# A fused pooled-attention and two-MLP kernel: chunk order, softmax subtraction on VectorE, and 24 idle weight steps

## The chip, the cores and the metric

The kernel runs on one core of one Trainium2 chip. The metric is the device time of one execution in microseconds; the number compared is the median over runs. The engines are named as the profile names them: PE is TensorE, DVE is VectorE, ACT is ScalarE, POOL is GpSimd, and SP is the queue that issues the DMAs.

## The reference

All data are float32. Keys and values are averaged over groups of 8 positions, attention runs over the 72 pooled positions, and the result passes through a gated MLP and an ELU MLP.

```python
k_p = k.reshape(B, H, Sp, pool, D).mean(axis=3)          # B 8, H 8, S 576, pool 8, Sp 72, D 64
v_p = v.reshape(B, H, Sp, pool, D).mean(axis=3)
scores = scale * np.matmul(q, k_p.transpose(0, 1, 3, 2))
scores = scores - np.max(scores, axis=-1, keepdims=True)
attn = np.exp(scores)
attn = attn / (np.sum(attn, axis=-1, keepdims=True) + 1e-09)
x = np.matmul(attn, v_p)                                 # -> (4608, 512)
gate = 1.0 / (1.0 + np.exp(-(x @ w_gate)))               # w_gate, w_val (512, 1536)
x = (gate * (x @ w_val)) @ w_out                         # w_out (1536, 512)
h = x @ w_in                                             # w_in (512, 2048)
g = np.where(h > 0.0, h, np.exp(np.minimum(h, 0.0)) - 1.0)
out = g @ w_out2                                         # w_out2 (2048, 512)
```

## The kernel before, in words

The MLP weights arrive as 64-bit words and are rebuilt on the chip as float32. Every float32 operand of a large product is then split into a rounded high half (an ACT copy) and a low half (a POOL or DVE subtraction), and a product is three matmul passes of those halves. The 4608 tokens are worked on in nine blocks of 512 (four tiles of 128). Each engine executes its instructions in the order in which the code emits them, so an instruction that waits holds up everything behind it on its engine.

**Block 0** does its attention first. Then comes the **chunk stage**: a loop over `c` from 0 to 5, each round handling one chunk of 128 columns of the first MLP for block 0, and beside it the attention of block 1, tile by tile. In a round PE does the scores of tile t (`emit_s`, name `ats`), the gate product (`gv`), the transposes of the softmax of the tile before (`emit_t`, name `att`), the value product (`gv`), the transposes of the next queries (`emit_q`, name `atq`) and the output products of the chunk before (`acc`). The names `ats`, `att` and `atq` share one PSUM place (tag `two`, one buffer of two banks): each must be read out before the next may be written. `convert(n)` takes n steps in the rebuilding of the first MLP's weights, each made of four DVE instructions (lines 116, 126, 130 and 120), an ACT copy and magnitude, and a POOL subtraction; there are three in a round.

The softmax of these tiles before the change: DVE finds the maximum of each head (line 612), ACT turns it into a bias (618) and then takes eight exponentials, one per head, straight from the PSUM bank (620). `emit_norm` then sums (DVE 628), adds a constant (ACT 636), inverts (DVE 637), scales the leftover window `pl` (DVE 640) and scales the whole tile (POOL 643).

After a stretch of gates for blocks 0 and 1 together comes the **bank stage**: the output products of block 1, with the attention of block 2 woven in by a hand-written table of half steps (`TURNS`, `put2`), through the same single `two` place.

The **middle stage** (blocks 2 to 8) runs seven products per half chunk: `u` counts half chunks from 0 to 11 and `k` the seven products. The product k=1 (`s2`) and the product k=3 (`s1`) write the same bank, and between them DVE must add the former into `u2` (line 1419). At even `u` the key sums of a later block (`pool_k`, line 490) are emitted at k=0. `WORK_AT` lists the places (u, k) where one step of the generator `prepared` is taken; it rebuilds the second MLP's weights (DVE lines 116 to 130 and 351 to 356, ACT copies and the magnitude at line 308, POOL subtractions, stores to DRAM from tiles named `nt`). Blocks 3 to 8 take the softmax in another form: DVE subtracts the maximum from the bank into SBUF (lines 598 and 599) and ACT takes one exponential in place (1206).

After block 8 the second MLP runs to the end.

Of the kernel before, what the change touches and what calls it, by code (L numbers as in the profile page):

```python
# [12 lines left out]
AF = mybir.ActivationFunctionType  # L13
# [11 lines left out]
def fused_kernel(  # L25
# [267 lines left out]
    def prepared():  # L293
# [44 lines left out]
        for q in range(C2 // 2):  # L338
# [31 lines left out]
            yield  # L370
            yield
            magnitude(i + 2)
# [7 lines left out]
        for i in range(C2, len(loads)):  # L380
            steps = narrowing(i)
            next(steps)
            if last is not None:
                keep(i - 1, *last)
            yield
            yield from steps
            fetch(i + 2)
            last = plain_t().bitcast(F32), tiles[i].bitcast(F32)
            apart(*last)
            yield  # L390
            magnitude(i + 1)
            yield
# [210 lines left out]

    peaks = {}

    def emit_s(t, p=None):
        a = two_banks("ats")
        scores(a, t, range(HP), q_t.pop(t))
        p = wts.tile([P, HK], F32, name="p0", tag="tt", bufs=2) if p is None else p
        sc = a[:, :, 0:4 * SP].rearrange("p a (h k) -> p a h k", k=SP)  # L610
        mx = at_p.tile([P, H], F32, name="mx", tag="mx", bufs=2)
        nc.vector.tensor_reduce(out=mx.rearrange("p (a h) -> p a h", a=2), in_=sc, op=ALU.max, axis=AX.X)
        peaks[t] = sc, mx
        return p

    def emit_exp(t, p):
        sc, mx = peaks.pop(t)
        nc.scalar.activation(out=mx, in_=mx, func=AF.Copy, scale=-SCALE)
        for h in range(H):
            nc.scalar.activation(  # L620
                out=p[:, h * SP:(h + 1) * SP], in_=sc[:, h // 4, h % 4], func=AF.Exp, scale=SCALE, bias=mx[:, h:h + 1]
            )
# [177 lines left out]
    with tc.manual_schedule():  # L800
# [43 lines left out]

        def scored(t):
            emit_s(t, ph[t])
            emit_exp(t, ph[t])

        for c in range(3):
# [5 lines left out]
        emit_k(0)  # L855
        scored(0)
        emit_q(3, qt[:, 3])
        scored(1)
        for t in range(2, TPW):
            scored(t)  # L860
            emit_norm(t - 2, ph[t - 2])
# [46 lines left out]
        for c in range(LAG_FROM):  # L908
            t = TPW + c - 1
            p = emit_s(t) if 0 < c <= TPW else None  # L910
            if c == 0:
                convert(1)
            gps = emit_gate(x0, c, 0)
            if c == 0:
                emit_k(1)
            if p is not None:
                emit_exp(t, p)
            sg = emit_sig(gps)
            if c:
                convert(1)  # L920
            if p is not None:
                emit_norm(t, p)
            if 1 < c <= TPW + 1:
                emit_t(t - 1)
            vps = emit_gate(x0, c, 1)
            if c < TPW:
# [3 lines left out]
            convert(1)  # L930
            g = emit_g(sg, vps)
            for op in post[c]:
                op()
# [91 lines left out]
        for i, (hq, hs, ht) in enumerate(TURNS):  # L1025
# [3 lines left out]
            put2(hs, s2, t)  # L1029
            put2(hs + 1, lambda t=t: emit_exp(t, p2[t]))  # L1030
            put2(hs + 2, lambda t=t: emit_norm(t, p2[t]))
# [172 lines left out]

        def exp_thin(p):
            nc.scalar.activation(out=p, in_=p, func=AF.Exp, scale=SCALE)

        halves_of = {}
# [15 lines left out]
        def thin_plan(m):  # L1224
# [9 lines left out]
            for i in range(TPW):  # L1234
# [4 lines left out]
                put(u + 1, 1, ready, AF.Exp)  # L1239
                put(u + 1, 2, lambda t=t: exp_thin(p_new[t]))  # L1240
                put(u + 1, 3, ready, AF.Sigmoid)
# [32 lines left out]
        SHAPE_AT = (0, 3)  # L1274
        WORK_AT = {(u, k) for u in range(2, C1, 2) for k in (0, 2, 3, 4, 5, 6)}
        WORK_AT |= {(u, k) for u in range(3, C1, 2) for k in (2, 4)}
# [422 lines left out]
```

## Time and profile before

| What | Value |
|---|---|
| median of three runs | 1864.53 us (1863.04 to 1865.72) |
| the profiled execution, its own time | 1861.72 us |
| its span, first to last instruction | 1859.9 us |
| PE busy in the span | 1783.1 us, 96% |
| DVE, ACT, POOL busy | 1082.1, 870.7 and 638.9 us |
| mean granted TensorE clock | 0.992 of full speed |

The profiled execution lies 1.8 us above its span and 2.8 us under the median. PE is busy for nearly the whole span, so the shares of busy time tell little; the stretches in which PE is not busy are what a reader looks for, and they lie in the first 330 us and in blocks 2 to 5.

### The profile page before, as it was taken

How to read it: one execution, taken by the hardware profiler on the slowest of the kernel's cores; microseconds unless marked ns; L12 is line 12 of the kernel's file. 1: busy time of each engine (PE TensorE's matmuls, PEld its weight loads, DVE VectorE, ACT ScalarE, POOL GpSimd, SP SyncE). 2: the span in 40 equal slices, each digit the busy share in tenths (PEclk: the TensorE clock that was granted, in tenths of full speed). 3: DMA queues.
4: the chain of work that ended last, by engine and by line, in shares of the span. 5: the costliest groups of instructions: out<-in, count | busy, mean ns of one | idle time of the engine just before them, and what ended most of it. 6: DMA issues, size and time to landing. Idle time of an engine off the chain costs nothing. (4 is left out here: it accounts for less than half of the span.)

```text
span 1859.9 us, 28508 instructions
## 1 busy us (share of the span) xinstructions
PE 1783.1 (96%) x10308; PEld 1581.6 (85%) x10308; DVE 1082.1 (58%) x2041; ACT 870.7 (47%) x1871; POOL 638.9 (34%) x626
## 2 busy tenths in 40 slices
PE   6679997999999999999999999999999999999999
PEld 5568776898988888899898989999999899999997
DVE  5687975776876767777664454345344444443432
ACT  4553444554544545455453244454444544544443
POOL 2354555443443434344332222222222222222222
PEclk9889999999999999999999999999999999999999
DMA  7345556876858677687666765353343343433431
GB/s 211 122 136 173 190 171 231 279 264 223 270 196 270 232 241 257 199 285 259 218 209 226 265 224 189 119 187 119 119 183 106 131 166 112 182 117 138 153 119 54
DMA packets 160013, 351.05 MB, mean 189 GB/s; under 512 B 48512, under 2 KB 86400, under 8 KB 159872
## 3 DMA queue, kind: packets, MB, share of 16 engines
q1 hardware_dynamic: 159872, 349.22, 55.1%
q8 instruction: 82, 1.34, 0.3%
q14 instruction: 59, 0.48, 0.1%
HBM read 288.88 MB, written 60.29 MB: 188 GB/s over the span
## 5 line engine op out<-in xcount | busy, mean ns | idle before, releaser
L1530 PE MATMUL bank<-form,wr 128*128 128x384 f32 x2016 | 411.0, 338 | 1.0 <-DVE u L1563 0.7
L1530 PEld LDWEIGHTS bank<-form,wr 128*128 128x128 f32 x2016 | 366.5, 188 | 29.1 <-DVE u L1563 1.1
L738 PE MATMUL acc<-g,wos 128*128 128x512 f32 x1128 | 354.3, 398 | 1.0 <-ACT g L96 0.2
L1576 PE MATMUL oacc<-w2o,gc 128*128 128x512 f32 x1080 | 288.9, 393 | 0.4 <-POOL gc L97 0.4
L1576 PEld LDWEIGHTS oacc<-w2o,gc 128*128 128x128 f32 x1080 | 199.6, 187 | 30.4 <-POOL gc L97 0.8
L97 POOL TENSOR_TENSOR gc<-ea,gc 128x384 fp32r<-128x384 f32 x96 | 98.0, 1021 | 298.7 <-ACT gc L96 295.6
L738 PEld LDWEIGHTS acc<-g,wos 128*128 128x128 f32 x1128 | 184.4, 189 | 11.4 <-ACT g L96 2.8
L97 POOL TENSOR_TENSOR gc<-pair,gc 128x384 fp32r<-128x384 f32 x96 | 97.8, 1018 | 260.6 <-ACT gc L96 240.1
L97 POOL TENSOR_TENSOR g<-sg,g 128x512 fp32r<-128x512 f32 x98 | 135.3, 1398 | 102.4 <-ACT g L96 102.2
L1404 PEld LDWEIGHTS pl<-s,wg 128*128 128x128 f32 x1008 | 139.9, 189 | 26.9 <-DVE u L1419 13.0
L1404 PE MATMUL pl<-s,wg 128*128 128x256 f32 x1008 | 153.6, 287 | 8.9 <-DVE u L1419 7.5
L1404 PE MATMUL pl<-s,tt 128*128 128x256 f32 x1008 | 152.1, 287 | 3.7 <-DMA tt<-td 2.9
L1404 PE MATMUL pl<-a,wg 128*128 128x256 f32 x1008 | 152.6, 287 | 3.0 <-DVE xe L1098 2.9
L1404 PEld LDWEIGHTS pl<-a,wg 128*128 128x128 f32 x1008 | 137.7, 189 | 16.4 <-ACT r L1104 5.8
L1404 PEld LDWEIGHTS pl<-s,tt 128*128 128x128 f32 x1008 | 139.2, 190 | 14.6 <-DVE rt L1344 2.0
L96 ACT ACTIVATE g<-sg 128x512 fp32r<-128x512 f32 x98 | 61.7, 630 | 180.2 <-DVE sg L1444 144.1
L1576 PE MATMUL oacc<-w2p,gc 128*128 128x512 f32 x540 | 143.1, 393 | 0.0
L1576 PEld LDWEIGHTS oacc<-w2p,gc 128*128 128x128 f32 x540 | 99.8, 187 | 14.8
L1539 ACT ACTIVATE ea<-bank 128x384 f32<-128x384 f32 x48 | 23.6, 492 | 157.7 <-PE bank L1530 157.7
L1543 DVE SCALAR_TENSOR_TENSOR ea<-ea,bank 128x384 f32<-128x384 f32 x48 | 26.6, 554 | 117.2 <-ACT ea L1540 117.2
L709 PE MATMUL gv<-x,wg 128*128 128x512 f32 x288 | 77.4, 420 | 10.0 <-POOL wg L97 6.0
L1539 ACT ACTIVATE pair<-pair 128x384 f32<-128x384 f32 x48 | 25.2, 525 | 129.6 <-DVE pair L1560 129.6
(223 smaller groups left out, 3059.5 us busy)
## 6 DMA issues: line engine op xcount, KB each, us to landing
wr<-wd SPq DMA_DIRECT2D x96, 896.0 KB, 5.2
tt<-td SPq DMA_DIRECT2D x84, 768.0 KB, 4.8
wos<-wd SPq DMA_DIRECT2D x94, 512.0 KB, 5.4
rw<-in_moe_w_out_dram SPq DMA_DIRECT2D x22, 512.0 KB, 3.7
td<-tw SPq DMA_DIRECT2D x36, 256.0 KB, 3.3
r<-yd SPq DMA_DIRECT2D x24, 384.0 KB, 8.2
out_dram<-po SPq DMA_DIRECT2D x36, 256.0 KB, 2.0
rw<-in_moe_w_in_dram SPq DMA_DIRECT2D x16, 512.0 KB, 7.1
```

The costliest lines, as they stand in the source:

```text
L96: nc.scalar.activation(out=dst_hi, in_=src, func=AF.Copy)
L97: eng.tensor_tensor(out=dst_lo, in0=src, in1=f32(dst_hi), op=ALU.subtract)
L709: nc.tensor.matmul(d, lhsT=w[:, i, a_w, j], rhs=x[j][:, a_x], start=(j == 0 and a_w == 0 and a_x == 0), stop=(j == KD - 1 and a_w == 1),)
L738: return lambda: nc.tensor.matmul(acc[m], lhsT=w[:, a_w, m * P:(m + 1) * P], rhs=g[:, a_g], start=(first and a_w == 0 and a_g == 0), stop= ...
L1404: nc.tensor.matmul(src, lhsT=w(a_w, j), rhs=f_t[nm][:, j, a_x], start=opens and m == 0, stop=m == 5, skip_group_check=True,)
L1530: nc.tensor.matmul(bank[b ^ flip], lhsT=wp[q][a_w][:, w, j * P:(j + 1) * P], rhs=form_tile(s, a)[j][:, a_x], start=opens and n == 0, stop= ...
L1539: nc.scalar.activation(out=e, in_=src, func=AF.Relu, scale=-1.0)
L1543: nc.vector.scalar_tensor_tensor(out=e, in0=e, scalar=-1.0, in1=src, op0=ALU.add, op1=ALU.max)
L1576: return lambda: nc.tensor.matmul(acc[t + i], lhsT=g[c][:, a_g, i * P:(i + 1) * P], rhs=wo2[2 * q + e][a_w], start=opens and p == 0, stop= ...
```

## The change

It has four parts.

1. In the chunk stage the order of a round is new. From c=2 on, the transposes of the former tile's softmax come first, then the gate product, a `convert`, the scores, the sigmoid, the value product, the exponential and the next queries; `emit_norm` now stands behind `emit_g`.
2. `emit_s` (block 1 and block 2) subtracts the maximum on DVE from the bank into SBUF, in one instruction of 128x576 elements, and `emit_exp` is one ACT instruction in place. The eight exponentials from the bank stay for block 0 only, under the name `straight`.
3. `prepared` loses 24 steps in which it did nothing: one in each of the 8 column pairs and one in each of the 16 row chunks.
4. `WORK_AT` loses the place k=0 at the five even `u`: 38 places in a block instead of 43.

```diff
@@ prepared()
             fetch(i + 3)
             yield
             yield
-            yield
             magnitude(i + 2)
             yield
...
             apart(*last)
-            yield
             magnitude(i + 1)
             yield
@@ emit_s, emit_exp
     def emit_s(t, p=None):
         a = two_banks("ats")
         scores(a, t, range(HP), q_t.pop(t))
         p = wts.tile([P, HK], F32, name="p0", tag="tt", bufs=2) if p is None else p
+        off_peak(p, a, 2)
+        return p
+
+    def emit_exp(p):
+        nc.scalar.activation(out=p, in_=p, func=AF.Exp, scale=SCALE)
@@ for c in range(LAG_FROM):
             t = TPW + c - 1
-            p = emit_s(t) if 0 < c <= TPW else None
-            if c == 0:
+            if c > 1:
+                emit_t(t - 1)
+            if c < 2:
                 convert(1)
             gps = emit_gate(x0, c, 0)
             if c == 0:
                 emit_k(1)
+            if c > 1:
+                convert(1)
+            p = emit_s(t) if 0 < c <= TPW else None
+            sg = emit_sig(gps)
+            vps = emit_gate(x0, c, 1)
             if p is not None:
-                emit_exp(t, p)
-            sg = emit_sig(gps)
-            if c:
-                convert(1)
-            if p is not None:
-                emit_norm(t, p)
-            if 1 < c <= TPW + 1:
-                emit_t(t - 1)
-            vps = emit_gate(x0, c, 1)
+                emit_exp(p)
             if c < TPW:
                 emit_q(t + 1)
             if c == 0:
                 sums_of("v", 1)
             convert(1)
             g = emit_g(sg, vps)
+            if p is not None:
+                emit_norm(t, p)
             for op in post[c]:
                 op()
@@ WORK_AT
-        WORK_AT = {(u, k) for u in range(2, C1, 2) for k in (0, 2, 3, 4, 5, 6)}
+        WORK_AT = {(u, k) for u in range(2, C1, 2) for k in (2, 3, 4, 5, 6)}
```

On PE, one round of the chunk stage before (the round c=3; `ats` are scores, `gv` the gate and then the value product, `att` the softmax transposes, `atq` the query transposes, `acc` the output products):

```order
L586 MATMUL ats<-kbd_140,qT 128x144 x4
L709 MATMUL gv<-x,wg_810 128x512 x12
L650 MATMUL att<-ident,p_735 128x128 x4
L650 MATMUL att<-ident,pl 128x128
L709 MATMUL gv<-x,wg_810 128x512 x12
L578 MATMUL atq<-ident,q_173 128x128 x4
L738 MATMUL acc<-g,wo_762 128x512 x12
```

and the round c=3 of the change:

```order
L651 MATMUL att<-ident,p_762 128x128 x4
L651 MATMUL att<-ident,pl 128x128
L710 MATMUL gv<-x,wg_789 128x512 x12
L584 MATMUL ats<-kbd_140,qT 128x144 x4
L710 MATMUL gv<-x,wg_789 128x512 x12
L576 MATMUL atq<-ident,q_173 128x128 x4
L739 MATMUL acc<-g,wo_746 128x512 x12
```

The transposes moved from behind the gate product to the head of the round, and the scores from the head to between gate and value. The number of matmuls is the same.

On DVE, from the maximum of the tile in round c=3 to the split of the transposes (`mx` the maxima, `sm` and `pl` the norm, `pt` the transposes; lines 116 to 130 are weight conversion), before:

```order
L612 TENSOR_REDUCE mx<-ats 128x8
L126 SCALAR_TENSOR_TENSOR nt<-rwo,nt 128x512
L116 TENSOR_SCALAR nt<-nt 128x512
L130 SCALAR_TENSOR_TENSOR nt<-rwo,nt 128x512
L120 TENSOR_SCALAR nt<-nt 128x512
L628 TENSOR_REDUCE sm<-p_855 128x8
L637 RECIPROCAL sm<-sm 128x8
L640 TENSOR_TENSOR pl<-p_855,sm 128x128
L105 TENSOR_TENSOR pt<-att,pt 128x4x128
L105 TENSOR_TENSOR pt<-att,pt 128x128
```

and in the change, up to the norm of the same round:

```order
L596 TENSOR_REDUCE mx<-ats 128x8
L597 TENSOR_TENSOR p_875<-ats,mx 128x576
L126 SCALAR_TENSOR_TENSOR nt<-rw,nt 128x512
L116 TENSOR_SCALAR nt<-nt 128x512
L130 SCALAR_TENSOR_TENSOR nt<-rw,nt 128x512
L120 TENSOR_SCALAR nt<-nt 128x512
L728 TENSOR_TENSOR sg<-sg,gv 128x512
L629 TENSOR_REDUCE sm<-p_875 128x8
L638 RECIPROCAL sm<-sm 128x8
L641 TENSOR_TENSOR pl<-p_875,sm 128x128
```

The subtraction into `p` is new behind the maxima, the product of sigmoid and value (`sg<-sg,gv`) now stands ahead of the norm, and a conversion stands between the maxima and both.

On DVE in the middle stage, block 5, around the start of the half chunk u=4 (`ks` are the key sums at k=0, line 1419 is the addition that frees the bank for k=3), before:

```order
L1448 TENSOR_TENSOR u2_2721<-u2_2721,pl2_2720 128x256
L1449 TENSOR_TENSOR sg_6913<-sg_6913,u2_2721 128x256
L490 TENSOR_REDUCE ks_7134<-rkv_7009 128x64
L355 TENSOR_TENSOR nt_7084<-nt_6957 128x256
L356 TENSOR_TENSOR nt_6818<-nt_7084,nt_6818 128x256
L1419 TENSOR_TENSOR u2_2721<-u2_2721,pl1_2719 128x256
L1222 TENSOR_TENSOR pt_6883<-att_7128,pt_6883 128x4x128
L1424 TENSOR_TENSOR u3_2722<-u2_2721,pl2_2720 128x256
```

and in the change at the same place:

```order
L1442 TENSOR_TENSOR u2_2665<-u2_2665,pl2_2664 128x256
L1443 TENSOR_TENSOR sg_6841<-sg_6841,u2_2665 128x256
L488 TENSOR_REDUCE ks_7061<-rkv_6940 128x64
L1413 TENSOR_TENSOR u2_2665<-u2_2665,pl1_2663 128x256
L1216 TENSOR_TENSOR pt_6811<-att_7055,pt_6811 128x4x128
L1418 TENSOR_TENSOR u3_2666<-u2_2665,pl2_2664 128x256
L120 TENSOR_SCALAR nt_6984<-nt_6984 128x512
L1421 TENSOR_TENSOR sg_7045<-u3_2666,pl1_2663 128x256
L126 SCALAR_TENSOR_TENSOR nt_6984<-rw2_6886,nt_6984 128x512
```

The two weight instructions between the key sums and the addition into `u2` are gone from there; another step of the weight work now stands after the products k=2 and k=3. Counted over the whole stage, the generator before ends at u=8 of block 7 and in the change at u=10 of block 7. In the change the magnitude of a column pair (line 308 before) stands two places behind the store of its buffer instead of three; in blocks 2, 3 and 4 this happens once each within one half chunk (u=6, u=10 and u=4).

## Rows read from the trace of the kernel before

**Rows 1.** Windows: stretch, its length, busy us (count) by engine, clock, DMA, GB/s.

```profile
60.20:142.80 82.60, 59.16 (x252) 46.62 (x253) 67.78 (x96) 47.29 (x102) 41.50 (x31) 0.88 0.43 140
...
266.70:327.40 60.70, 48.99 (x268) 39.02 (x269) 36.66 (x61) 30.64 (x91) 30.57 (x27) 1.00 0.64 217
327.40:995.80 668.40, 654.18 (x4602) 590.10 (x4602) 479.14 (x1010) 334.15 (x717) 262.86 (x267) 1.00 0.73 241
```

**Rows 2.** Waits, chunk stage: waiter <- releaser, us, times, longest us.

```profile
PE att L650 <- ACT p L620: 14.3, 3, 6.3
...
DVE sm L637 <- ACT sm L636: 9.4, 4, 2.3
...
DVE sm L628 <- ACT p L620: 5.2, 4, 1.5
```

**Rows 3.** Timeline of PE, chunk stage: start, us, instruction, idle before it.

```profile
106.69 1.12 PE L650 MATMUL att<-ident,p 128*128 128x128 f32 x4 [3.19 <-ACT p L620]
...
142.82 0.76 PE L671 MATMUL atv<-pt,vbd 128*128 128x64 f32 x6
```

**Rows 4.** Timeline of ACT, chunk stage, round c=3.

```profile
104.83 1.80 ACT L620 ACTIVATE p<-ats,mx 128x72 f32<-128x72 f32 x8
```

**Rows 5.** Groups by line and shape, whole span: busy us, mean ns, idle before.

```profile
L599 DVE TENSOR_TENSOR p<-ats,mx 128x288 f32<-128x288 f32 x48 | 22.0, 457 | 1.7
...
L612 DVE TENSOR_REDUCE mx<-ats 128x8 f32<-128x576 f32 x12 | 9.0, 753 | 8.7 <-PE ats L586 8.4 <-ACT p L620 0.3
```

**Rows 6.** Timeline of DVE, weight conversion in rounds c=2 and c=4.

```profile
98.05 0.68 DVE L126 SCALAR_TENSOR_TENSOR ntr<-rw,ntr 128x512 int32<-128x512 int32 x1
98.74 1.43 DVE L116 TENSOR_SCALAR nt<-nt 128x512 f32<-128x512 f32 x1
...
101.78 0.83 DVE L120 TENSOR_SCALAR nt<-nt 128x512 int32<-128x512 int32 x1
...
119.89 0.68 DVE L126 SCALAR_TENSOR_TENSOR ntr<-rw,ntr 128x512 int32<-128x512 int32 x1
...
121.42 0.42 DVE L120 TENSOR_SCALAR nt<-nt 128x512 int32<-128x512 int32 x1
```

**Rows 7.** Timeline of POOL beside the first of them.

```profile
98.22 1.67 POOL L97 TENSOR_TENSOR wg<-nt,wg 128x512 fp32r<-128x512 f32 x1 [2.51 <-ACT wg L96]
```

**Rows 8.** Waits of PE in the bank stage.

```profile
PE att L650 <- POOL g L97: 4.8, 2, 3.0
PE ats L586 <- ACT qT L579: 2.2, 2, 1.3
PE atq L578 <- ACT p L620: 1.4, 1, 1.4
...
PE att L650 <- ACT p L620: 1.3, 1, 1.3
```

**Rows 9.** Timeline, bank stage, around the second tile's exponentials: ACT, then PE.

```profile
281.65 0.26 ACT L491 ACTIVATE ks<-ks 128x64 f32<-128x64 f32 x1 [3.97 <-DVE ks L490]
...
283.08 1.80 ACT L620 ACTIVATE p<-ats,mx 128x72 f32<-128x72 f32 x8
...
284.98 0.63 PE L650 MATMUL att<-ident,p 128*128 128x128 f32 x4 [2.97 <-POOL g L97]
```

**Rows 10.** Waits of PE in blocks 2 to 7.

```profile
PE pl L1404 <- DVE u L1419: 7.5, 10, 2.1
```

**Rows 11.** Timeline of PE, middle stage: first and last of eight such waits.

```profile
363.86 0.98 PE L1404 MATMUL pl<-s,wg 128*128 128x256 f32 x6 [0.27 <-DVE u L1419]
...
740.69 0.98 PE L1404 MATMUL pl<-s,wg 128*128 128x256 f32 x6 [0.31 <-DVE u L1419]
```

**Rows 12.** Timeline of DVE, block 5, before the longest wait.

```profile
703.35 1.31 DVE L356 TENSOR_TENSOR nt<-nt 128x256 f32<-128x256 f32 x1
704.58 0.41 DVE L1419 TENSOR_TENSOR u<-u,pl 128x256 f32<-128x256 f32 x1
```

**Rows 13.** Timeline of ACT, block 2: a magnitude that waits for a store.

```profile
424.16 0.66 ACT L308 ACTIVATE nt<-rw 128x512 f32<-128x512 f32 x1 [1.67 <-DMA wd<-nt]
```

More of the change, by code (lines that the diff above doesn't have):

```diff
@@ L602, in off_peak @@
         )
-    peaks = {}
     def emit_s(t, p=None):
@@ L609, in emit_s, with straight @@
         p = wts.tile([P, HK], F32, name="p0", tag="tt", bufs=2) if p is None else p
+        off_peak(p, a, 2)
+        return p
+    def emit_exp(p):
+        nc.scalar.activation(out=p, in_=p, func=AF.Exp, scale=SCALE)
+    def straight(t, p):
+        a = two_banks("ats")
+        scores(a, t, range(HP), q_t.pop(t))
         sc = a[:, :, 0:4 * SP].rearrange("p a (h k) -> p a h k", k=SP)
@@ L612, in emit_s @@
         nc.vector.tensor_reduce(out=mx.rearrange("p (a h) -> p a h", a=2), in_=sc, op=ALU.max, axis=AX.X)
[L613 to L617, printed above, removed]
         nc.scalar.activation(out=mx, in_=mx, func=AF.Copy, scale=-SCALE)
@@ L843, in fused_kernel @@
         ph = [room[t // 3][:, t % 3 * HK:(t % 3 + 1) * HK] for t in range(TPW)]
-        def scored(t):
-            emit_s(t, ph[t])
-            emit_exp(t, ph[t])
         for c in range(3):
@@ L855, in fused_kernel @@
         emit_k(0)
-        scored(0)
+        straight(0, ph[0])
         emit_q(3, qt[:, 3])
-        scored(1)
+        straight(1, ph[1])
         for t in range(2, TPW):
-            scored(t)
+            straight(t, ph[t])
             emit_norm(t - 2, ph[t - 2])
@@ L1029, in fused_kernel @@
             put2(hs, s2, t)
-            put2(hs + 1, lambda t=t: emit_exp(t, p2[t]))
+            put2(hs + 1, lambda t=t: emit_exp(p2[t]))
             put2(hs + 2, lambda t=t: emit_norm(t, p2[t]))
@@ L1203, in s_thin @@
             off_peak(p_new[t][:, h * HK // 2:(h + 1) * HK // 2], a, 1)
-        def exp_thin(p):
-            nc.scalar.activation(out=p, in_=p, func=AF.Exp, scale=SCALE)
         halves_of = {}
@@ L1239, in thin_plan @@
                 put(u + 1, 1, ready, AF.Exp)
-                put(u + 1, 2, lambda t=t: exp_thin(p_new[t]))
+                put(u + 1, 2, lambda t=t: emit_exp(p_new[t]))
                 put(u + 1, 3, ready, AF.Sigmoid)
```

## Prediction

> **What bounds the kernel now.** I read the windows first, to find the stretches in which PE has free time; the page's totals hide them, since PE is busy for 96% of the span. Three stretches matter [rows 1]. In the chunk stage (60.2 to 142.8 us, where the products with the pooled values begin [rows 3]) PE is busy for 59.2 of 82.6 us, at a granted clock of 0.88, so the bound there is something else. In the bank stage (266.7 to 327.4) PE is busy for 49.0 of 60.7 us. In blocks 2 to 7 (327.4 to 995.8) it is busy for 654.2 of 668.4 us, so 14 us are open. Then I read the waits in each.
>
> In the chunk stage PE's largest wait is that of the softmax transposes on the exponentials of line 620: 14.3 us in three waits [rows 2]. The timeline shows why: the eight exponentials of round c=3 end at 104.83 + 1.80 = 106.63 us, and the transposes start at 106.69 [rows 3, 4]. The transposes write the place that the scores occupy, and the exponentials read the scores there. But taking away a wait of PE is worth only as much as the next engine allows, and that is DVE: busy 67.8 of 82.6 us, so 14.8 us idle, of which 9.4 us are waits of the inversion for ACT's small addition (line 636) and 5.2 us waits of the sum for the exponentials [rows 1, 2]. These two waits are what the stage can give back.
>
> In the bank stage PE waits 1.4, 1.3 and 4.8 us ahead of transposes, and 2.2 us for the query copies [rows 8]. The 4.8 us stand against POOL in the view, but the longer one ends at 284.98, right behind the exponentials that end at 283.08 + 1.80 = 284.88 [rows 9]; I count all three, 7.5 us, as waits for a bank that exponentials hold.
>
> In blocks 2 to 7 the largest wait is that on the addition of line 1419: 7.5 us in ten waits [rows 10]. I set each wait against the place (u, k) where it falls, by counting six matmuls to a product. Eight of the ten, with 6.1 us, fall on k=3 of an even u at whose k=0 a weight step gave DVE work; the first and the last are shown [rows 11]. The longest shows the queue: the subtraction of line 356 takes 1.31 us and ends at 704.66, and the addition starts at 704.58 right behind it [rows 12].
>
> **The change, part by part.** *Chunk stage, what it takes off DVE.* The sum no longer follows the exponentials directly: it now stands behind a conversion and the product with the value, so the exponential (started after the subtraction) is done by then. I take the 5.2 us as gone. The inversion waited 2.3 us at most, 9.4 in four, because ACT had a table load, the sigmoid, a copy and a magnitude between the exponentials and its addition. In the new order ACT has only the high half of g ahead of it. I keep 0.3 us for each tile, 1.2 us; that is my choice between nothing and the 2.3 of now, near the low end because the g copy overlaps the sum.
>
> *What it adds to DVE.* Four subtractions of 128x576 out of the bank. There is no such row. Half the width takes 0.457 us, twice that is 0.91; the maximum over 128x576 takes 0.753 us [rows 5]. I take 0.75, since the maximum reads the same elements from the same bank: 4 x 0.75 = 3.0 us.
>
> *What it does to the conversions.* A set of four conversion instructions takes 119.89 to 121.84, so 1.95 us, when POOL is quiet, and 98.05 to 102.61, so 4.56 us, when it is not: the second instruction of the slow set takes 1.43 us, and the POOL subtraction that starts at 98.22 ends at 99.89 [rows 6, 7]. The difference is 2.6 us. POOL's 41.5 us of work [rows 1] will lie in a shorter stage, beside a DVE that idles less. I charge one more slow set in the stage, 2.6 us.
>
> The Trainium skill (SBUF — State Buffer, Who interferes with whom) says that VectorE and GpSimd share a pair of SBUF ports under an exclusive lock, and that the loser blocks for the whole instruction. The rows of the slow set agree with that. By that rule POOL's 41.5 us and fifteen quiet sets of 1.95 us add up to an estimated 71 us in the stage, which would limit the gain there to about 12 us.
>
> Sum for the stage: 5.2 + 9.4 - 1.2 - 3.0 - 2.6 = 7.8 us. The ends: DVE never idle and no more slow sets gives 14.8 - 3.0 = 11.8; one more slow set in each of the four rounds gives 14.6 - 1.2 - 3.0 - 10.4 = 0. The ACT side gets lighter (eight exponentials become one) and its table loads stay as many, two in a round. PE's busy time of 59.2 us fits into 74.8. What is late next is the norm: the transposes now open a round, so PE waits there for the POOL product of the round before. I cost that at nothing more, since DVE sets the length of a round; the wait is where PE's surplus will show.
>
> *Bank stage.* The bank is now freed by DVE's subtraction, 0.75 us behind the maximum, instead of by ACT 2 us and more later, so the 7.5 us lose their cause. They do not all come back. Behind the transposes stands an ACT copy, and ACT's queue is held by the copy of the key sums, which waits 3.97 us for DVE [rows 9], which in turn waits for loaded keys; no edit moves that load against the stage's start. And the 2.2 us of waits for the query copies [rows 8] come from that same chain and stay. I take half, 3.7 us, between 1.4 (only the one wait of the query transposes) and 7.5.
>
> *Middle stage.* With k=0 free of weight work, the addition of line 1419 follows the key sums directly, and the 6.1 us go. The steps move to other places, where the next product that needs DVE is further off. The other price is on ACT. With an idle step gone, a magnitude of the column pairs comes two places after the store of the buffer that it overwrites, not three. The trace has two such waits for a store on ACT; one is the 1.67 us at 424.16 [rows 13], and PE's loss from such a wait was about 0.7 us (the two of the ten waits that the even u do not explain, 7.5 - 6.1 = 1.4). In the new order three magnitudes stand two places behind within one half chunk. I charge one more such loss, 0.7 us: 6.1 - 0.7 = 5.4 us. The ends are 7.5, where all ten waits go, and a loss, which is a rival below. The 24 idle steps and the places taken out nearly balance (the work ends in block 7 before and after), so nothing is left over for after block 8.
>
> The sum is 7.8 + 3.7 + 5.4 = 16.9 us. Against the profiled execution's own 1861.7 us that gives 1844.8; the median is 2.8 us above it, so **1847.6 us**.
>
> **Rivals.** *The ceiling.* Every cause named goes and DVE's slow sets grow no more frequent: 11.8 + 7.5 + 7.5 = 26.8 us, so 1837.7. For it speaks that PE has slack in the first two stages; against it POOL's load beside the conversions.
>
> *The shared port.* The conversions take the time that the waits gave: with a slow set more in nearly every round the stage gains between 0 and 2.6 us. I take 1.3, and the sum is 1.3 + 3.7 + 5.4 = 10.4, so 1854.1. For it speaks that the slow sets take 2.3 times as long as the quiet ones; against it that the stage now has idle stretches of POOL and of DVE which need not fall together. The Trainium skill's lock (SBUF — State Buffer) is this mechanism.
>
> *The wait changes its name.* The transposes at the head of a round wait for the norm as long as they waited for the exponentials, 14.3 us in all, the weight work makes its waits at k=2 instead of k=0, and only 1.4 us of the bank stage is left: 1863.1, no change that can be told. Against it speaks that the bank was held by ACT behind a table load, which the norm's chain does not have.
>
> *Slower: the magnitudes.* The 23 magnitudes in blocks 2 to 7 that come behind a store in the ring of three buffers each hold ACT, and with it the copies that DVE and PE need. At 0.7 us each they cost 16.1 us and cancel the gain; it decides from about 0.8 us. At 1.4 us each, twice the loss seen, they cost 32.2 against 7.8 + 3.7 + 6.1 = 17.6: 1879.1. Against it speaks that only two of them waited before, and that the row chunks, which are most of them, still stand four steps behind their store (five before).
>
> **How the numbers follow.** The forecast has a chance of 0.54, the shared port 0.20, the ceiling 0.16, the changed name 0.06 and the slower case 0.04. The forecast's own range is 1842 to 1853. The range of 8 in 10 takes in the ceiling and the port and leaves the last two out: 1836 to 1857. A measurement of this kernel tells about 0.2% (3.7 us) from no change; the first three cases are all faster by more, so faster has 0.90, the same 0.06 and slower 0.04.
>
> **What would show it.** In the changed profile the stretch from the second round's head to the first products with the weighted values should be about 75 us instead of 82.6, and DVE nearly without idle time in it; PE's wait ahead of the softmax transposes should stand against POOL's norm, at 2 to 3 us a round. The subtraction should have a row of about 0.75 us, and the slow conversion sets should be no more than one or two above those of now. The waits for line 620 should be gone after block 0, and the wait for the query copies still there in the bank stage. The waits for the addition of line 1419 should drop to about 1.5 us, and ACT should show three or so waits of a magnitude for a store. The prediction is wrong if the conversions stretch (port), if a magnitude's wait holds PE for more than 0.8 us as a rule, or if the middle stage grows new waits behind weight steps at k=4 of odd u, where I counted none.

## The result, and the profile after

| | before | after |
|---|---|---|
| median of four runs each | 1865.12 us (1863.04 to 1866.41) | 1845.12 us (1844.00 to 1846.72) |
| ratio, 95% interval | | 0.9894 (0.9877 to 0.9912) |
| profiled execution: own time, span | 1861.72, 1859.9 us | 1844.74, 1843.0 us |
| DVE, ACT, POOL busy in the span | 1082.1, 870.7, 638.9 us | 1087.7, 860.8, 633.0 us |

The kernel is 20.0 us faster; 16.9 had been forecast, and the median is 2.5 us below the forecast's. The windows of the kernel after, cut as in [rows 1] (the first one starts 1.2 to 1.3 us behind the last value sums in both), show where:

```profile
59.20:135.60 76.40, 57.36 (x253) 45.30 (x254) 73.25 (x105) 43.81 (x73) 41.97 (x32) 0.87 0.46 154
259.10:317.80 58.70, 50.94 (x268) 40.18 (x269) 38.84 (x65) 25.09 (x59) 30.51 (x27) 0.97 0.68 232
317.80:978.40 660.60, 652.93 (x4601) 591.30 (x4601) 477.37 (x1010) 334.14 (x717) 256.69 (x267) 1.00 0.73 243
```

The chunk stage falls from 82.6 to 76.4 us, the bank stage from 60.7 to 58.7, the middle from 668.4 to 660.6. In the chunk stage DVE's idle time falls from 14.8 to 3.15 us (76.40 - 73.25) while its work grows by 5.5 (73.25 - 67.78): -11.7 + 5.5 = -6.2, the whole change of the stage. The waits of that stretch (waiter, releaser, us, times, longest) name what is left:

```profile
PE att L651 <- POOL p L644: 12.7, 4, 4.3
...
DVE sm L638 <- ACT sm L637: 2.4, 4, 1.0
```

DVE's wait for the exponentials, 5.2 us in [rows 2], has no row any more, and that for ACT's small addition is 2.4 instead of 9.4. PE's wait of 14.3 us for the exponentials is one of 12.7 for POOL's norm. The timeline of ACT in round c=3 shows how the maximum now leads to the exponential:

```profile
100.91 0.60 ACT L721 ACTIVATE sg<-gv 128x512 f32<-128x512 f32 x1
101.53 1.28 ACT L610 ACT_TABLE_LOAD   x1
103.63 0.69 ACT L610 ACTIVATE p<-p 128x576 f32<-128x576 f32 x1 [0.82 <-DVE p L597]
```

The table load runs while ACT has nothing else to do: only the exponential behind it waits for DVE. Before, the copy of the maximum (line 618) stood ahead of the load and waited, so that the load, from 103.53 to 104.81, lay between the maximum and the exponentials of [rows 4]:

```profile
103.31 0.21 ACT L618 ACTIVATE mx<-mx 128x8 f32<-128x8 f32 x1 [2.71 <-DVE mx L612]
103.53 1.28 ACT L620 ACT_TABLE_LOAD   x1
```

DVE's groups in the stage, the leftover window first, then the new subtraction:

```profile
L641 DVE TENSOR_TENSOR pl<-p,sm 128x128 f32<-128x128 f32 x4 | 4.9, 1220 | 0.1
...
L597 DVE TENSOR_TENSOR p<-ats,mx 128x576 f32<-128x576 f32 x4 | 3.0, 758 | 0.1
```

The same window took 575 ns before (the group of the kernel before):

```profile
L640 DVE TENSOR_TENSOR pl<-p,sm 128x128 f32<-128x128 f32 x4 | 2.3, 575 | 0.1
```

In the bank stage PE's waits for a bank that exponentials hold [rows 8] are gone. Those for the query copies grew from 2.2 to 3.6 us, and the one for the pooled keys' diagonal from 1.4 (line 507 before) to 1.9:

```profile
PE ats L584 <- ACT qT L577: 3.6, 3, 1.7
PE att L651 <- DVE kbd L505: 1.9, 1, 1.9
```

In blocks 2 to 7 PE's waits for the addition, 7.5 us in [rows 10] (line 1413 now), are down to 0.5, while three waits for line 1435, 1.2 us in all, are new:

```profile
PE pl L1398 <- DVE xe L1095: 2.5, 6, 0.5
PE pl L1398 <- DVE sg L1435: 1.2, 3, 0.6
PE pl L1398 <- DVE u L1413: 0.5, 2, 0.3
PE pl L1398 <- DVE u L1437: 0.5, 1, 0.5
```

One profile of a stage is not exact. Over the profiled executions that share a stage's code, its length scatters by 1 to 4 us, so means are used below. The stage ends are read from PE: the end of the last value sums, the first product with weighted values, the first key transposes of the bank stage, the first and the first block-8 product of the middle. The expectations of the first four runs count the chunk stage from the start of the last group of value sums, which makes it 1.9 us longer in each kernel (85.8 and 79.5 us instead of 83.9 and 77.6).

| stage, us | old code: mean (executions) | new code: mean (executions) | difference | forecast |
|---|---|---|---|---|
| chunk | 85.2 (83.9, 86.6, 85.2) | 77.2 (77.6, 76.9, 77.0) | -8.1 | -7.8 |
| bank | 61.3 (60.7 to 62.6, 5) | 57.4 (56.5 to 58.7, 8) | -3.9 | -3.7 |
| middle | 669.4 (668.1 to 670.9, 5) | 662.8 (660.7 to 664.6, 8) | -6.6 | -5.4 |

The sum is -18.6, against 20.0 by the medians; the rest lies within the interval.

### The profile page after: what moved, and what is told of

Its sections match the earlier page's. It is cut to its first block, busy times and chain, and to the rows that moved or that the text cites. A ratio compares the mean times of both kernels' runs of the same rounds, so it can differ in the third digit from the quotient of the medians.

```text
span 1843.0 us, 28452 instructions
## 1 busy us (share of the span) xinstructions
PE 1780.2 (97%) x10308; PEld 1581.3 (86%) x10308; DVE 1087.7 (59%) x2049; ACT 860.8 (47%) x1807; POOL 633.0 (34%) x626
## 3 DMA queue, kind: packets, MB, share of 16 engines
q8 instruction: 82, 1.34, 0.3%
## 5 line engine op out<-in xcount | busy, mean ns | idle before, releaser
L97 POOL TENSOR_TENSOR g<-sg,g 128x512 fp32r<-128x512 f32 x98 | 127.6, 1320 | 102.8 <-ACT g L96 102.7
L1570 PEld LDWEIGHTS oacc<-w2p,gc 128*128 128x128 f32 x540 | 99.8, 187 | 14.8
L1548 DVE TENSOR_TENSOR u<-p,bank 128x384 f32<-128x384 f32 x48 | 26.6, 554 | 97.5 <-PE bank L1524 96.5
```

What stands on the lines that cost most here:

```text
L97: eng.tensor_tensor(out=dst_lo, in0=src, in1=f32(dst_hi), op=ALU.subtract)
L1548: nc.vector.tensor_tensor(out=u2, in0=t_p1, in1=src, op=ALU.add)
L1570: return lambda: nc.tensor.matmul(acc[t + i], lhsT=g[c][:, a_g, i * P:(i + 1) * P], rhs=wo2[2 * q + e][a_w], start=opens and p == 0, stop= ...
```

## The experiments

Every median below stands beside one of the kernel before from the same chip. **Theory A** at the start was the prediction's reading: the new order takes the waits off DVE, and the subtraction only costs DVE time in the chunk stage.

**The order alone**: part 1 of the change, with the old exponentials and the old table.

```diff
+            if c > 1:
+                emit_t(t - 1)
...
+            if p is not None:
+                emit_exp(t, p)        # still eight, from the bank
```

> Part 1 of the change alone: the new order of a round in the chunk stage; the eight exponentials still read the bank, and the weight steps are as before. Theory A (DVE's queue sets the length of a round; the gain comes from the order, which takes the waits of the sum and of the inversion off DVE, and the subtraction only costs DVE time): the chunk stage, from the last matmul of the value sums to the first product with the pooled values, takes 76 to 78 us (85.8 before, 79.5 in the change), shorter than in the change because the four subtractions of 0.76 us are missing; the total falls by 7 to 10 us. Theory B (the shared PSUM place that the exponentials hold sets it, and the subtraction is what frees it): 84 to 86 us, and no gain. Both: bank stage 60.7 us and blocks 2 to 7 668 us as before.

Measured: 1864.57 beside 1864.72 us, ratio 0.9999 (0.9987 to 1.0012); chunk stage 85.2 us, the old code's mean. Theory A fell here. ACT in round c=3, then the stage's waits:

```profile
107.75 0.21 ACT L618 ACTIVATE mx<-mx 128x8 f32<-128x8 f32 x1 [1.18 <-DVE mx L612]
107.97 1.28 ACT L620 ACT_TABLE_LOAD   x1
109.27 1.80 ACT L620 ACTIVATE p<-ats,mx 128x72 f32<-128x72 f32 x8
```

```profile
PE att L650 <- POOL p L643: 12.1, 4, 3.6
...
DVE sm L637 <- ACT sm L636: 7.8, 4, 2.3
...
PE atq L578 <- ACT p L620: 4.9, 3, 2.1
...
DVE sm L628 <- ACT p L620: 2.7, 4, 0.9
...
DVE mx L612 <- PE ats L586: 1.6, 3, 0.8
```

The order takes 4.1 us of the 14.6 us of DVE's two waits, not 13.4. It pays for them with new waits of DVE for the scores (1.6 us) and at the leftover window, which goes from 2.3 to 5.2 us:

```profile
L640 DVE TENSOR_TENSOR pl<-p,sm 128x128 f32<-128x128 f32 x4 | 5.2, 1310 | 0.1
```

**The softmax form alone**: part 2, in the old order and with the old table.

```diff
+        off_peak(p, a, 2)
+        return p
+
+    def emit_exp(p):
+        nc.scalar.activation(out=p, in_=p, func=AF.Exp, scale=SCALE)
```

> Part 2 alone: the maximum is subtracted on DVE and one exponential is taken in place, in the order of before, with the weight steps of before. Theory A: the chunk stage stays at 84 to 87 us, because DVE still waits behind ACT for its inversion, 9 us in all, and has 3 us more to do; PE's wait for the bank goes, but only into other waits. Theory B: 79 to 80 us, as in the change. Both: the bank stage takes 58 to 59 us instead of 60.7, blocks 2 to 7 668 us. Total: A 1861 to 1865, B 1856 to 1858.

Measured: 1854.68 us, ratio 0.9950 (0.9932 to 0.9969); chunk stage 78.6 us, bank stage 56.5. The form by itself takes 6.7 of the 8.1 us of the chunk stage and the whole gain of the bank stage. Waits, then the window's group, at its old price:

```profile
DVE sm L640 <- ACT sm L639: 5.2, 4, 1.3
```

```profile
L643 DVE TENSOR_TENSOR pl<-p,sm 128x128 f32<-128x128 f32 x4 | 2.3, 587 | 0.1
```

**The table and the idle steps alone** (parts 3 and 4), and **the order and the form without them** (parts 1 and 2), divide the change in two.

> Parts 3 and 4 alone: 24 idle steps and the places k=0 at even u taken out; attention as before. Theory (the waits for the addition of line 1419 sat behind weight steps at k=0): blocks 2 to 7 take 660 to 662 us instead of 668.4, the waits for that addition fall from 7.5 to about 1 us, total about 1857. Rival (the middle stage gained because it started earlier and its loads met other traffic): 667 to 669 us and no gain.

> Parts 1 and 2 without 3 and 4. If the parts add up: chunk stage 79.5, bank stage 58.7, blocks 2 to 7 668 us with the waits of 7.5 us for the addition of line 1419 (or its counterpart), total 1853 or so. If the stages depend on each other, blocks 2 to 7 differ from 668 us by more than 3.

Measured: parts 3 and 4, 1857.56 us, ratio 0.9958 (0.9947 to 0.9970), middle stage 661.9; parts 1 and 2, 1853.31 us, ratio 0.9942 (0.9922 to 0.9962), middle stage 670.9, chunk stage 76.9. The two gains, 7.2 and 11.4 us, make 18.6 of the 20.0, so the halves add up. The order on top of the form takes 1.7 us off the stage (78.6 to 76.9), which is within the scatter of single executions.

What does the form take away? **Theory C**: ACT's chain between the maximum and the inversion, in which the table load could not start before the maximum's copy. **Theory B**: the bank, which the eight reads hold. The next two runs move the table load alone.

**An early table load in the kernel before.**

```diff
...
             if p is not None:
+                nc.scalar.activation(out=spare[:, 1:2], in_=spare[:, 0:1], func=AF.Exp)
                 emit_exp(t, p)
```

> The kernel before with a tiny ScalarE exponential on a constant tile ahead of the maximum's copy in the four rounds of the chunk stage, so that the table load runs while ScalarE waits for the maximum. Nothing else changes: eight exponentials out of the banks, the old order, the old table. Theory C: the exponentials and all behind them on ScalarE come 1.28 us earlier in each round; VectorE's four waits for the exponentials fall from 5.2 us to 0 to 1, those for the sum's copy stay at about 9.4; the chunk stage goes from 83.9 to 79 to 80 us, the kernel to about 1860. Theory B (it is the banks and the eight reads that count): the waits change their name, the chunk stage keeps within 1.5 us of 83.9, the kernel within 1.5 us of 1865.

Measured: 1860.29 beside 1865.60 us, ratio 0.9973 (0.9964 to 0.9982); chunk stage 80.9 us, 4.3 under the old code's mean and 2.9 under the profile before. ACT, then DVE's waits:

```profile
97.67 1.28 ACT L919 ACT_TABLE_LOAD   x1
98.96 0.20 ACT L919 ACTIVATE spare<-spare 128x1 f32<-128x1 f32 x1
101.97 0.21 ACT L618 ACTIVATE mx<-mx 128x8 f32<-128x8 f32 x1 [2.81 <-DVE mx L612]
102.21 1.80 ACT L620 ACTIVATE p<-ats,mx 128x72 f32<-128x72 f32 x8
```

```profile
DVE sm L637 <- ACT sm L636: 9.1, 4, 2.3
...
DVE sm L628 <- ACT p L620: 0.5, 2, 0.2
```

The waits for the exponentials go from 5.2 to 0.5 us and those for the addition stay, as theory C had it; the stage came out 1 to 2 us above its range. The banks are held by eight reads as before, so their hold does not explain this part.

**A late table load in the kernel after**: a copy that waits for the subtraction, ahead of the exponential.

```diff
...
             if p is not None:
+                nc.scalar.activation(out=spare[:, 0:1], in_=p[:, 0:1], func=AF.Copy)
                 emit_exp(p)
```

> The changed kernel with one tiny ScalarE copy (128x1, reading the shifted scores) ahead of the exponentials of the four rounds of the chunk stage; it is a Copy that waits for the subtraction, so the load of the exponentials' table falls behind the subtraction instead of ahead of it. The scores' banks still come free at the subtraction. Theory C (the gain of the chunk stage is what was taken out of ScalarE's chain between the maximum and the inversion, of which the table load is 1.28 us a round): ScalarE comes about 1.5 us later to the sum's copy in each round, VectorE's waits for it grow from 2.4 us in four to 6 to 8, the chunk stage goes from 77.6 to 81 to 83 us, and the kernel is 4 to 6 us above the changed one, near 1850. Theory B (the gain comes from the banks' early release and from fewer ScalarE instructions; the table load lies in slack): the chunk stage stays within 1 us of 77.6, the kernel within 1.5 us of the changed one.

Measured: 1847.57 us, ratio 0.9909 (0.9894 to 0.9924), so 2.5 us above the changed kernel's median (the intervals of the two ratios overlap); chunk stage 80.4 us, 3.2 above the new code's mean. ACT, then the waits:

```profile
106.14 0.20 ACT L921 ACTIVATE spare<-p 128x1 f32<-128x1 f32 x1 [1.97 <-DVE p L597]
106.36 1.28 ACT L610 ACT_TABLE_LOAD   x1
107.66 0.69 ACT L610 ACTIVATE p<-p 128x576 f32<-128x576 f32 x1
```

```profile
DVE sm L638 <- ACT sm L637: 4.8, 4, 1.3
...
DVE mx L596 <- PE ats L584: 1.5, 1, 1.5
```

The direction is theory C's, the size half of it: of 4 x (1.28 + 0.20) = 5.9 us put into the chain, DVE shows 2.4 more at the inversion and 1.5 at the next maximum; the rest shows in no wait of DVE. The table load is therefore worth some 3 to 4 us of the form's 6.7 in this stage. The rest goes with the form's other differences, one exponential of 0.69 us for eight of 1.80 and the bank freed by DVE; no run separates these two.

**The gate product first.** Is PE's wait of 12.7 us for the norm on the path? The kernel after, with the first gate product ahead of the transposes.

```diff
-            if c > 1:
-                emit_t(t - 1)
...
             gps = emit_gate(x0, c, 0)
...
             if c > 1:
+                emit_t(t - 1)
                 convert(1)
```

> The changed kernel with the first half of the gate product put ahead of the former tile's transposes on TensorE in rounds 2 to 4 (VectorE's and ScalarE's own order barely moves). Theory (VectorE bounds the chunk stage and TensorE's 12.7 us of waits ahead of the transposes cost nothing): those waits fall to under 3 us, the wait appears elsewhere on TensorE, VectorE stays without idle, and the chunk stage stays within 1.5 us of 77.6. Rival (TensorE's wait is on the path, since what VectorE converts depends on the transposes): the chunk stage falls by 4 us or more.

Measured: 1846.42 us, ratio 0.9901 (0.9885 to 0.9918); chunk stage 77.3 us, unchanged. PE's waits:

```profile
PE ats L584 <- DVE pt L105: 8.5, 3, 2.8
...
PE att L651 <- POOL p L644: 1.5, 1, 1.5
```

The wait changed its place (12.7 us became 8.5 and 1.5), and nothing was won. PE's wait at the head of the round was surplus, as the prediction had costed it.

**More work for POOL.** The kernel after, with a subtraction of the gate tile done twice, to the same result, in four rounds.

```diff
                 emit_norm(t, p)
+                nc.gpsimd.tensor_tensor(out=g[:, 1], in0=sg, in1=f32(g[:, 0]), op=ALU.subtract)
```

> The changed kernel with the gate tile's low half computed a second time (the same subtraction, the same result) on GpSimd behind the normalization in the four rounds of the chunk stage: 1.2 to 1.7 us more of GpSimd's work a round beside VectorE, for which nobody waits. Theory (GpSimd's elementwise passes slow VectorE's passes beside them, and VectorE bounds the stage; this is the term of 2.6 us for a further slow set in the forecast): one conversion set more reads slow in most rounds, VectorE's busy time grows by 3 to 5 us over the stage, the chunk stage goes from 77.6 to 80 to 83 us, the kernel to 1848 to 1851. Rival (GpSimd works beside VectorE at no cost, the slow sets have another cause): the stage stays within 1 us of 77.6.

Measured: 1848.38 us, ratio 0.9916 (0.9899 to 0.9932), 3.3 us above the changed kernel's median (the intervals overlap here too); chunk stage 79.6 us, 2.4 above the new code's mean and 0.4 short of the range. The window of the stage:

```profile
60.20:139.70 79.50, 57.60 (x252) 45.35 (x253) 75.92 (x103) 44.26 (x73) 48.34 (x35) 0.89 0.43 146
```

POOL's 5.8 us more (four subtractions of 1.46) made the stage 2.4 us longer, some 0.4 us for each microsecond of POOL's. DVE is as dense as before (3.6 us idle of 79.5), and its conversion instructions take 0.893 us on average, 0.832 in the kernel after. These rows fit the mechanism of the shared-port rival; the price is under half of POOL's time.

**The idle steps alone**, with the places of the weight steps as before.

```diff
             yield
-            yield
             magnitude(i + 2)
...
             apart(*last)
-            yield
             magnitude(i + 1)
```

> The kernel before with the idle steps alone taken out (table with the places k=0 kept, the old order and the old exponentials). Theory (the gain of 7.7 us in the middle stage is the places': eight waits of TensorE for the gate tile): the middle stage stays at 666 to 669 us, the eight or so waits of 0.9 us for the gate tile stay, the kernel at 1863 to 1866. Rival (the magnitude that starts a step sooner brings weights sooner and is worth the 2.3 us by which the forecast fell short): the middle stage falls to 665 or under, the kernel to about 1862.

Measured: 1862.54 us, ratio 0.9987 (0.9977 to 0.9996); middle stage 667.4 us, 1.9 under the mean of the old code and 1.0 under the profile before. The median lies 0.5 us under the theory's range, the middle stage inside it. The waits on the addition are half of what they were, which neither theory had:

```profile
PE pl L1402 <- DVE u L1417: 3.8, 9, 1.4
```

Taking both, places and idle steps, removes 6.6 us, so about 5 belong to the places and 1 to 2 to the idle steps; a closer division is within the scatter.

**The key sums' copy on DVE.** In the bank stage of the kernel after, the ACT copy of the later block's key sums is a DVE copy.

```diff
+        if by_dve:
+            nc.vector.tensor_copy(out=t[:n, 1], in_=t[:n, 0])
+        else:
             nc.scalar.activation(out=t[:n, 1], in_=t[:n, 0], func=AF.Copy)
...
```

> The changed kernel with the copy of the key sums of the later block, in the bank stage, done by VectorE instead of ScalarE. Theory (what was left of the forecast's 3.7 us in the bank stage hangs on ScalarE: its copies stand ahead of the queries' copy, for which TensorE still waits 3.6 us there): that wait falls to 1 to 2 us and bank and middle stage together fall from 719.4 to 716 to 718 us. Rival (the stage's end, and the middle's steps behind it, are set by the arrival of the weights or by VectorE, and a wait removed from ScalarE comes back): bank and middle together stay within 1.5 us of 719.4, or rise as VectorE gets the copies.

Measured: 1843.96 us, ratio 0.9894 (0.9879 to 0.9908), the ratio of the change itself. Bank and middle stage together take 720.7 us, 719.4 without the edit. PE's waits in the bank stage:

```profile
PE acc L742 <- DMA wos<-wd: 2.9, 3, 1.3
...
PE ats L587 <- ACT qT L580: 0.6, 1, 0.6
```

The wait for the query copies goes from 3.6 to 0.6 us, as asked, and waits for transfers take its place (2.9 us, against 0.4 in the kernel after). The rival held: what is left in this stage was not the copy's to give.

**A straight form without the chain's faults.** If theory C is the whole story, the old form should win once its table load is early and its sums come from ACT, since DVE then has two passes less a round.

```diff
+                bias=mx[:, h:h + 1], accum_out=sm[:, h:h + 1]
...
+                nc.scalar.activation(out=spare[:, 1:2], in_=spare[:, 0:1], func=AF.Exp)
+                exp_sum(t, p)
```

> The changed kernel with another softmax in the four rounds of the chunk stage alone: the exponentials again straight from the banks, eight of them with the negative maximum as bias, each writing its head's sum as it goes, so that neither the subtraction (0.76 us) nor the sum (0.75 us) is VectorE's, and the sum's copy stands right behind them on ScalarE; a tiny exponential ahead of the maximum's copy brings the table load into ScalarE's wait, as in the experiment with the early load. Bank stage and middle keep the form of the changed kernel. Theory C (the old form lost by its chain on ScalarE; with the load out of the chain and two passes less on VectorE, which bounds the stage, the straight form wins): VectorE's busy time falls by 5 to 6 us, its waits for the reciprocal's input grow by no more than 2 us, the chunk stage goes from 77.6 to 73 to 75 us, the kernel to 1841 to 1843. Rival B (the banks held through the eight reads and the longer ScalarE work cost what VectorE saves): the chunk stage stays at 77 to 80 us, the kernel at 1844 to 1848.

Measured: 1847.71 us, ratio 0.9915 (0.9900 to 0.9930); chunk stage 81.6 us, outside both ranges. DVE's work fell as foreseen, from 73.8 to 67.1 us, and its wait grew (window, then wait):

```profile
58.20:139.80 81.60, 59.06 (x254) 45.99 (x254) 67.09 (x98) 52.92 (x143) 41.63 (x31) 0.87 0.44 143
```

```profile
DVE sm L660 <- ACT sm L659: 11.7, 4, 3.4
```

The expectation had put the sums' copy right behind the exponentials; the code left it behind four other ACT instructions. The next kernel moves it there.

```diff
         sums[t] = sm
+        nc.scalar.activation(out=sm, in_=sm, func=AF.Copy, bias=1e-9)   # in exp_sum
...
-        nc.scalar.activation(out=sm, in_=sm, func=AF.Copy, bias=1e-9)   # in emit_norm
```

> The experiment with the exponentials' own sums, with one edit more: the copy that adds the small constant to the sums moved from the place of the normalization to right behind the eighth exponential on ScalarE, where the former expectation had it by mistake; there it stood behind the queries' copy, two weight copies and the gate tile's copy, and VectorE waited 11.7 us for it in four rounds, with 67.1 us of work in a stage of 81.6. Theory C (ScalarE's chain from the maximum to the inversion sets the stage once VectorE has less work; 2.8 us of it a round are the four copies in between): those waits fall from 11.7 to under 3 us, the stage from 81.6 to 72 to 75 us, below the changed kernel's 77.6, and the kernel to 1840 to 1843. Rival (the eight reads and their sums, 2.5 us a round from the banks on ScalarE, are themselves the chain, and a wait for them, for the queries or for the former tile's transposes takes over): the stage stays at 77 to 80 us, the kernel at 1844 to 1847.

Measured: 1849.60 beside 1865.94 us, ratio 0.9914 (0.9901 to 0.9928); chunk stage again 81.6 us, outside both ranges. The wait is down from 11.7 to 1.7 us, and the stage has not moved:

```profile
DVE pt L105 <- ACT pt L103: 6.2, 4, 1.9
...
DVE sm L666 <- ACT sm L633: 1.7, 3, 0.6
```

PE, then POOL, in round c=3 show what took over:

```profile
108.41 0.66 PE L576 MATMUL atq<-ident,q 128*128 128x128 f32 x4 [1.13 <-ACT p L629]
...
114.63 0.65 PE L679 MATMUL att<-ident,p 128*128 128x128 f32 x4 [2.81 <-POOL p L672]
```

```profile
110.30 1.31 POOL L97 TENSOR_TENSOR wg<-nt,wg 128x512 fp32r<-128x512 f32 x1 [8.30 <-ACT wg L96]
111.56 1.46 POOL L97 TENSOR_TENSOR g<-sg,g 128x512 fp32r<-128x512 f32 x1
112.98 1.59 POOL L672 TENSOR_TENSOR p<-p,sm 128x576 f32<-128x576 f32 x1
```

The query transposes wait for the bank that the eight reads hold; the query copy, a weight copy and two POOL subtractions queue behind that, then the norm, then the next round's transposes. From the maximum's end at 105.32 (it starts at 104.56 and takes 0.76) to these transposes are 9.3 us; in the kernel after it is 7.3 (102.80 to 110.09). The query transposes start 3.1 us behind the maximum here (105.32 to 108.41) and 1.1 us in the kernel after (102.80 to 103.91), which is the whole of the difference. Here DVE, with 67 us of work in 81.6, no longer bounds the stage: the loop through ACT and POOL does, and the eight reads lie in that loop. ACT itself is busy with them until the bank comes free, so these rows do not part the bank's hold (theory B) from ACT's own time; a run that frees the bank early with ACT's own sums, which would show it alone, was not made. No version beat the changed kernel by more than the runs can tell.

## Why the prediction was right, and where not

*The bound of the chunk stage* was read rightly: DVE's idle time was what could be had, and PE's wait behind the norm cost nothing (the run with the gate product first).

*The cause given for it was wrong.* The step "in the new order ACT has only the high half of g ahead of it" put DVE's 13.4 us of waits down to the order. The order alone gave nothing; the softmax form alone gave 6.7 of 8.1 us. What the prediction lacked lies just ahead of the exponentials of its [rows 4]: ACT's chain behind the maximum, with a copy that waits and the table load behind it, worth 3 to 4 us by the two runs that move the load. It said of ACT that its table loads "stay as many", which is true; what changed is that the load can run ahead of the wait. On top of the form the order takes the inversion's wait from 5.2 to 2.4 us, and the leftover window takes 2.6 us back. That the stage's sum came out, 7.8 beside 8.1 us, is luck as far as the cause goes: the gain put down to the order came from the form, and both are in the change.

*Terms of that stage.* The sum's wait went whole (5.2). Of the inversion's 9.4 us, 2.4 stayed where 1.2 had been chosen. The four subtractions took 3.0 us (0.758 each, 0.75 forecast). The term of 2.6 us for one more slow conversion set has the right size and the wrong place: the conversion instructions took 0.866 us each before and 0.832 after (58.0 us in 67 of them and 59.1 in 71, by the groups of lines 116 to 130 in the stage), while the leftover window went from 2.3 to 4.9 us. The window took 1.16 to 1.31 us wherever the new order stood with the sums' copy in its place, whichever the softmax form, and 0.57 to 0.59 with the old order; in the last run, where it meets an idle POOL, 0.29. In the kernel after the window of round c=3 starts at 107.24 and ends at 108.43, and POOL's subtraction beside it runs from 107.00 to 108.28. Before, the window ran from 110.00 to 110.58, beside the end of a subtraction of POOL's that ran from 109.14 to 110.43. Both windows end 0.15 us behind POOL: the order moved the window from the end of a weight's subtraction to the start of the subtraction of g. The Trainium skill (SBUF — State Buffer, Who interferes with whom) gives a lock of the shared ports held for the whole instruction; these rows agree, and the run with more work for POOL shows that by no means every POOL instruction is paid for by DVE.

*Bank stage*: forecast 3.7, measured 2.0 in the profile after and 3.9 by the means. The softmax form was the cause (the form alone 56.5 us, the order alone 62.6). A table load stands there only ahead of the first tile's exponentials (273.07), so for the other three tiles it is not the load; that it is the bank, and not ACT's shorter work, is argued and not shown. The half that was kept back was right: the query copy's wait stayed, and when it was taken away, transfers took its place.

*Middle stage*: forecast 5.4, measured 7.7 in the profile after and 6.6 by the means, all of it from the table and the idle steps (670.9 us without them). Two pieces were mis-sized. The waits for the addition went from 7.5 to 0.5 us, not by 6.1, nearly the bound of 7.5. And the magnitudes' further wait for a store, 0.7 us, was not paid: where ACT had two such waits with 5.3 us in blocks 2 to 7, it now has one:

```profile
  DMA wd<-nt: 1.7, 1
```

The run with the idle steps alone shows them to help, not to cost. The slower rival had no support in any run. These two pieces, 0.9 and 0.7 us, are 1.6 of the 2.5 us by which the median lies below the forecast; the remainder is less than the scatter of a stage. Two things lay outside the prediction. The new waits for line 1435, 1.2 us, stand where it had put the moved steps at nothing (the run with the idle steps alone has them too, the one without parts 3 and 4 has not). And there is PE's wait for a transfer (`tt<-td`), 1.1 us before and none in this profile, but 0.8 and 2.1 us in two other runs of the same middle code, so it is no gain to count on.

## What to carry to other kernels

Before a gain is put down to an order, follow the chain on the engine that is waited for: which of its instructions carries the wait, and what must come behind it. An activation whose table load has to follow a waiting copy pays for the load on the path; in the form where the waiting instruction is the activation itself, or with a tiny activation ahead of the copy, the load is hidden. And when the engine that bounds a stage is relieved, look for the loop through the other engines that lies just under it: here a form that took 6.7 us of work off DVE made the stage 4.4 us longer, and the rows point to its eight reads, by the bank that they hold or by ACT's own time.

## What the runs showed of the hardware

A table load of 1.28 us starts as soon as ACT is free, ahead of the wait of the activation that needs it (101.53 in the kernel after, with the exponential at 103.63), and an activation that waits for nothing starts right behind it (in the run with the order alone 107.97 + 1.28, then 109.27): no further time for the switch shows. In all fourteen traces the loads take 1.283 us each and start 17 to 19 ns behind the ACT instruction before them. Eight exponentials that also write their sums took 2.5 us (105.75 to 108.28 in the first run with them) against 1.80 without. A DVE multiplication of 128x128 (the leftover window) took 0.29 us beside an idle POOL. Started inside a POOL subtraction, it ended 0.14 to 0.15 us behind that subtraction, in all 52 cases of the thirteen traces that have them in the chunk stage: after 0.56 to 0.61 us in the old order and 0.98 to 1.34 us in the new one.
